# A bucketed attention with two feed-forward layers: the first head pair scores into borrowed banks, under a new order of the work

## The chip, the cores and the metric

The kernel runs on one core of one Trainium2 chip. A core has five engines that work side by side: TensorE (PE) multiplies matrices, VectorE (DVE) and ScalarE (ACT) work element by element and read its results from the PSUM banks, GpSimd (POOL) works element by element in SBUF alone in this kernel, and SyncE (SP) issues the transfers. The metric is the device time of one launch in microseconds (us), lower is better.

## The reference, cut to what matters

```python
# q, k, v: (2, 8, 768, 64); proj: (64, 6)
q_bits = (np.einsum('bhsd,dk->bhsk', q, proj) > 0)      # k_bits alike
q_bucket = np.sum(q_bits * 2 ** np.arange(6), axis=-1)  # k_bucket alike
mask = q_bucket[:, :, :, None] == k_bucket[:, :, None, :]
scores = np.where(mask, (1 / np.sqrt(64)) * q @ k.T, -1e9)
attn = np.exp(scores - scores.max(-1, keepdims=True))
attn = attn / (attn.sum(-1, keepdims=True) + 1e-09)
x = (attn @ v)                       # heads side by side: (1536, 512)
h = x @ w_in                         # first layer, d_ff 2048
x = (h * (1 / (1 + np.exp(-h)))) @ w_out
out = ((x @ w1) * (x @ w2)) @ w3 @ w_out2    # second layer, d_ff 1024
```

## The kernel before, in words

**Attention.** The 16 heads are taken as 8 pairs. For each head there are NQ = 6 groups of 128 queries against 768 keys. A group has four steps. TensorE scores it into a score tile of two PSUM banks (`scores`, L772, and `scores_lone`, L782, for the first pair, where `lone` is true and where one call scores the same group of both heads). VectorE takes the negated maximum (`peak`, L792), ScalarE exponentiates into `P` and sums the rows into a column of `sums` (`exp`, L797), and VectorE transposes `P` in blocks of 32 (`swap`, L817). When all twelve groups of a pair are transposed, TensorE weights V with them in six steps (`weigh`, L830) that take all four single banks, two called W and two called R, and the result is moved out (`move`, L849). The row sums go over TensorE (`flip`, L865), ScalarE (`unload`, L868) and VectorE (`invert`, L872) to DRAM and back as a row for every partition, and `norm` (L892) multiplies by it.

**Banks.** There are eight PSUM banks. Two score tiles of two banks each are the pool S (L381 and L382). The two tiles `turn` are the pool R (L380 and L383): the sign projections, the flips and half of the weighting use them. The two tiles `acc` are the pool W (L384): the products of the combined weights, the early steps of the first layer, half of the weighting, and 24 fillers (`warm`, L583) of three transpositions each, which compute nothing and only keep TensorE at work. After the last pair `hand_over` (L970) closes the attention's pools and gives six more banks to W.

**Weights.** Each weight comes as 64-bit words in loads of 512 KB and is made into a pair of rounded value and rest by `low`, `high`, `join`, `hi` and `lo` (`piece`, L416). During the attention w3 and the last output matrix are multiplied into one (`product`, L914): eight matrices in eight steps each, of three matmuls each.

**Layers.** `rise` and `fall` are the steps of the two layers, three matmuls each; 24 rising and 8 falling steps of the first layer are done during the attention, all others after it.

**The order.** Nothing is issued as the code is written. Each `op` call records an operation with its engines, its dependencies, the buffers it takes and gives back, and a number of the list PLACE: the first call takes the first number and so on (L254). `Plan.run` (L263) then plays the operations through with assumed durations and issues, on each engine, the one that can start first; among several of these the one with the smallest number. Buffers of S are given out in the order of the numbers, those of W and R to whoever comes (`FREE_FOR_ALL`, L241).

Of the kernel before, what the change touches and what calls it, by code (L numbers as in the profile page):

```python
# [37 lines left out]
WINDOWS = ((0, 1), (1, 1), (2, 2), (3, 2), (4, 2))  # L38
WARM, WARM_GAP = 24, 1.6
# [3 lines left out]
    220, 21, 22, 23, 19, 24, 28, 29, 90, 101, 53, 93, 91, 248, 325, 328, 326, 46, 48, 50, 43, 124, 128, 210, 199, 223,  # L43
    224, 221, 225, 17, 49, 11, 31, 18, 4, 8, 240, 13, 171, 191, 275, 348, 68, 14, 2, 232, 243, 242, 0, 6, 1, 57, 5, 132,
    9, 552, 7, 186, 45, 97, 163, 263, 121, 394, 164, 293, 125, 200, 168, 302, 129, 304, 54, 3, 241, 185, 38, 519, 245,
    116, 95, 270, 122, 689, 271, 123, 295, 318, 153, 333, 267, 170, 264, 190, 300, 197, 280, 201, 189, 208, 188, 211,
    137, 133, 203, 265, 829, 460, 234, 247, 148, 294, 515, 244, 246, 235, 60, 126, 127, 400, 414, 207, 425, 438, 173,
    175, 26, 27, 317, 327, 103, 104, 99, 96, 15, 71, 179, 182, 288, 277, 365, 363, 368, 369, 135, 174, 331, 154, 339,
    209, 337, 161, 298, 268, 334, 213, 251, 284, 338, 214, 413, 283, 379, 229, 407, 336, 381, 238, 352, 146, 344, 383,
    236, 372, 347, 384, 256, 395, 350, 393, 359, 392, 354, 399, 360, 450, 358, 420, 373, 434, 361, 426, 375, 447, 405,  # L50
    355, 464, 343, 310, 512, 1122, 586, 1129, 592, 1034, 607, 158, 144, 377, 314, 977, 290, 518, 534, 228, 155, 205,
    349, 353, 215, 206, 1077, 70, 452, 257, 269, 330, 291, 176, 222, 282, 279, 409, 401, 237, 233, 230, 231, 181, 262,
    487, 485, 415, 402, 634, 638, 631, 629, 459, 378, 429, 382, 443, 380, 430, 387, 457, 386, 445, 397, 568, 404, 453,
    412, 391, 406, 463, 417, 533, 418, 478, 441, 547, 106, 437, 483, 461, 467, 431, 496, 455, 1069, 440, 498, 465, 320,
    475, 504, 462, 1217, 486, 505, 466, 664, 491, 508, 477, 690, 490, 633, 489, 650, 591, 659, 590, 670, 570, 680, 628,
    691, 411, 469, 422, 494, 538, 863, 819, 830, 312, 82, 621, 872, 877, 136, 342, 1266, 134, 507, 296, 219, 289, 509,
    306, 305, 520, 517, 666, 661, 319, 376, 322, 316, 484, 456, 555, 482, 763, 751, 1085, 1088, 1100, 1098, 332, 497,
    530, 479, 597, 492, 554, 480, 617, 502, 559, 511, 470, 510, 569, 563, 651, 500, 574, 564, 444, 579, 587, 565, 436,
    56, 571, 580, 585, 667, 581, 602, 624, 656, 605, 606, 644, 558, 609, 674, 647, 543, 654, 688, 648, 693, 665, 706,
    702, 695, 432, 39, 802, 37, 780, 40, 812, 52, 811, 55, 1474, 59, 476, 748, 261, 677, 982, 149, 915, 934, 20, 1807,  # L60
    167, 1064, 1066, 195, 458, 1056, 341, 733, 421, 10, 906, 1052, 506, 499, 626, 622, 166, 774, 216, 192, 165, 193,
    632, 794, 699, 701, 752, 845, 852, 850, 870, 873, 44, 681, 719, 703, 760, 678, 708, 716, 791, 683, 734, 723, 827,
    726, 747, 861, 825, 729, 754, 867, 856, 728, 766, 880, 841, 107, 757, 782, 893, 789, 758, 798, 919, 732, 736, 785,
    898, 657, 761, 801, 972, 370, 779, 807, 974, 542, 772, 817, 1047, 710, 876, 945, 875, 949, 838, 965, 1619, 984,
    1638, 999, 1846, 1013, 1111, 1126, 797, 687, 892, 76, 1472, 1482, 759, 1120, 1238, 1495, 1497, 366, 523, 778, 2124,
    1394, 1193, 809, 1726, 1755, 764, 859, 718, 712, 1157, 1148, 427, 424, 416, 423, 1102, 1001, 810, 744, 1276, 1382,
    671, 673, 639, 669, 813, 796, 818, 1048, 840, 828, 885, 1357, 1167, 832, 901, 1440, 777, 831, 890, 1446, 755, 835,
    904, 1459, 1026, 866, 921, 1513, 1042, 16, 902, 960, 1514, 851, 905, 967, 1526, 1171, 912, 990, 1547, 998, 918, 993,
    1542, 324, 938, 996, 1549, 1242, 929, 1023, 1621, 1227, 1007, 1859, 1073, 1967, 1067, 1979, 1092, 1991, 1090, 2009,
    1005, 2000, 1220, 1831, 981, 844, 1104, 1632, 1453, 1470, 1620, 983, 1589, 2021, 2017, 620, 776, 578, 1006, 1596,  # L70
    1605, 2102, 1624, 1174, 1492, 1247, 846, 843, 1499, 1488, 942, 944, 927, 936, 1527, 1391, 1270, 1264, 2263, 1984,
    1375, 1367, 1124, 1125, 1780, 953, 1025, 1622, 971, 957, 1061, 1704, 1168, 966, 1070, 1715, 911, 973, 1065, 1705,
    903, 989, 1071, 1769, 1286, 1003, 1083, 1752, 1260, 1703, 1008, 1093, 1796, 1194, 1011, 1105, 1799, 1268, 1017,
    1399, 1827, 1246, 1015, 1429, 1813, 1080, 1033, 1431, 1828, 446, 1021, 1441, 1868, 641, 969, 1366, 1019, 1401, 2294,
    1400, 2242, 1411, 2233, 1427, 1068, 1438, 1853, 1854, 73, 963, 1086, 398, 1805, 1818, 1215, 922, 1493, 2527, 2590,
# [1280 lines left out]
```

## Time and profile before

| | |
|---|---|
| median of 3 runs | 714.15 us (712.88 to 716.6) |
| the profiled execution's own time | 713.73 us |
| its span, first to last instruction | 711.9 us |
| TensorE busy | 679.1 us, 95% |
| VectorE busy | 531.2 us, 75% |
| ScalarE busy | 375.4 us, 53% |
| mean granted clock of TensorE | 0.969 |

The times of the parts below are those of the profiled execution. A busy share says how much of a stretch an engine had an instruction running; matmuls overlap, so a busy TensorE need not be at its peak. The granted clock is the share of TensorE's 2.4 GHz that it was given; 0.50 is 1.2 GHz. In rows of the trace PE is TensorE's matmuls and PEld its weight loads, a bracket gives the idle time of the engine before the first instruction of the row and what ended it.

### The profile page before, as it was taken

How to read it: one execution, taken by the hardware profiler on the slowest of the kernel's cores; microseconds unless marked ns; L12 is line 12 of the kernel's file. 1: busy time of each engine (PE TensorE's matmuls, PEld its weight loads, DVE VectorE, ACT ScalarE, POOL GpSimd, SP SyncE). 2: the span in 40 equal slices, each digit the busy share in tenths (PEclk: the TensorE clock that was granted, in tenths of full speed). 3: DMA queues.
4: the chain of work that ended last, by engine and by line, in shares of the span. 5: the costliest groups of instructions: out<-in, count | busy, mean ns of one | idle time of the engine just before them, and what ended most of it. 6: DMA issues, size and time to landing. Idle time of an engine off the chain costs nothing.

```text
span 711.9 us, 14222 instructions
## 1 busy us (share of the span) xinstructions
PE 679.1 (95%) x5792; PEld 551.2 (77%) x5792; DVE 531.2 (75%) x744; ACT 375.4 (53%) x694; POOL 249.5 (35%) x243
## 2 busy tenths in 40 slices
PE   8699797999999999899999999999999999999997
PEld 5477586777887887678888888888888888878886
DVE  7887988888796996797876788687877446483555
ACT  5664866565675785465753545444735465231220
POOL 3735776586754631347020040005321043020000
PEclk9869699999999999999999999999999999999999
DMA  8444766475563563200340231102200041100004
GB/s 261 135 158 141 193 175 168 128 182 164 165 171 97 140 190 115 89 1 1 102 133 2 90 117 58 33 31 89 60 29 1 1 147 46 44 1 1 0 16 162
DMA packets 22881, 68.33 MB, mean 96 GB/s; under 512 B 3872, under 2 KB 4640, under 8 KB 22304
## 3 DMA queue, kind: packets, MB, share of 16 engines
q1 hardware_dynamic: 22816, 67.43, 31.7%
q8 instruction: 45, 0.74, 0.4%
q14 instruction: 20, 0.16, 0.1%
HBM read 55.58 MB, written 5.29 MB: 86 GB/s over the span
## 4 chain that ended last, share of the span: by engine, by line
PE 54%; DVE 4%; ACT 1%; issue 0%
PE more L1245 21%; PE more L1081 13%; PE more L1201 7%; PE acc L1081 6%; PE acc L1245 4%; PE acc L1201 3%; DVE y L407 1%; DVE gl L407 1%; DVE X L1264 1%; DVE X L1020 0%; ACT y L400 0%; DVE sg L1147 0%; ACT gh L400 0%; ACT xm L442 0%; DVE more L1098 0%
## 5 line engine op out<-in xcount | busy, mean ns | idle before, releaser
L1081 PE MATMUL more<-y,piece 128*128 128x512 f32 x432 | 110.0, 389 | 0.0
L799 ACT ACTIVATE P<-score,st 128x768 f32<-128x768 f32 x96 | 85.7, 896 | 45.1 <-DVE st L793 42.7
L793 DVE TENSOR_REDUCE st<-score 128x1 f32<-128x770 f32 x96 | 88.0, 946 | 24.2 <-PE score L777 20.6
L1245 PE MATMUL more<-gh,piece 128*128 128x512 f32 x312 | 105.3, 389 | 0.1
L1264 DVE SCALAR_TENSOR_TENSOR X<-more,X 128x512 f32<-128x512 f32 x101 | 68.2, 687 | 39.3 <-PE more L1245 38.7
L818 DVE STREAM_TRANSPOSE pt<-P 128x768 f32<-128x768 f32 x96 | 90.0, 964 | 9.0 <-ACT P L799 8.6
L1081 PEld LDWEIGHTS more<-y,piece 128*128 128x128 f32 x432 | 81.1, 188 | 16.9
L836 PE MATMUL turn<-pt,V 32*64 32x193 f32 x1536 | 74.9, 334 | 5.1 <-issue 5.1
L836 PE MATMUL acc<-pt,V 32*64 32x193 f32 x1536 | 75.9, 334 | 2.8 <-issue 2.6
L836 PEld LDWEIGHTS acc<-pt,V 32*64 32x64 f32 x1536 | 59.3, 134 | 11.9 <-issue 9.5
L1245 PEld LDWEIGHTS more<-gh,piece 128*128 128x128 f32 x312 | 58.6, 188 | 12.6 <-DVE X L1264 0.5
L836 PEld LDWEIGHTS turn<-pt,V 32*64 32x64 f32 x1536 | 56.7, 134 | 7.7 <-issue 7.1
L457 DVE SCALAR_TENSOR_TENSOR x<-x,x 128x512 uint32<-128x512 uint32 x60 | 48.4, 810 | 17.2 <-ACT x L442 16.6
L1245 PE MATMUL more<-gl,piece 128*128 128x512 f32 x156 | 60.8, 390 | 0.4 <-DVE gl L407 0.4
L777 PE MATMUL score<-ka,qa 128*128 128x384 f32 x168 | 51.4, 389 | 8.6 <-ACT P L799 7.6
L1201 PE MATMUL more<-x,piece 128*128 128x512 f32 x216 | 55.0, 389 | 0.0
L1081 PE MATMUL acc<-y,piece 128*128 128x512 f32 x198 | 52.8, 391 | 0.1
L447 ACT ACTIVATE x<-raw 128x512 uint32<-128x512 uint32 x43 | 28.9, 673 | 38.8 <-DVE piece L407 16.4
L918 PE MATMUL acc<-piece,piece 128*128 128x512 f32 x192 | 48.9, 397 | 0.4 <-ACT X L855 0.4
L777 PEld LDWEIGHTS score<-ka,qa 128*128 128x128 f32 x168 | 30.1, 204 | 23.6 <-ACT P L799 14.3
L1245 PE MATMUL more<-piece,gh 128*128 128x512 f32 x152 | 47.1, 391 | 0.4 <-DVE sg L1098 0.2
L1201 PEld LDWEIGHTS more<-x,piece 128*128 128x128 f32 x216 | 40.5, 188 | 8.4
(191 smaller groups left out, 1338.6 us busy)
## 6 DMA issues: line engine op xcount, KB each, us to landing
raw<-in_w SPq DMA_DIRECT2D x25, 512.0 KB
raw<-in_wo SPq DMA_DIRECT2D x22, 512.0 KB
raw<-in_win SPq DMA_DIRECT2D x15, 512.0 KB
V<-in_v SPq DMA_DIRECT2D x16, 384.0 KB
rawm<-in_w SPq DMA_DIRECT2D x7, 512.0 KB
kraw<-in_kT SPq DMA_DIRECT2D x8, 384.0 KB
qraw<-in_qT SPq DMA_DIRECT2D x8, 384.0 KB
invb<-inverse SPq DMA_DIRECT2D x16, 192.0 KB
```

The lines of the kernel that those rows point to most:

```text
L447: nc.scalar.activation(out=u32(t), in_=pair(raw)[:, :, 0], func=AF.Copy, scale=0.875 * 2.0 ** -29, bias=0.49)
L457: engine[e].scalar_tensor_tensor(out=u32(x), in0=u32(x), scalar=3, in1=u32(t), op0=ALU.logical_shift_left, op1=ALU.bitwise_or)
L777: nc.tensor.matmul(out=sc[:, g, :HF], lhsT=lhs[:k, qs], rhs=rhs[:k, g * HF:g * HF + HF], start=(k == 128), stop=(k != 128),)
L793: nc.vector.tensor_reduce(out=plan[uk("st")][:, 0:1], in_=plan[uk("S")][:, :, :HF + 1], op=ALU.max, axis=AX.XY, negate=True)
L799: nc.scalar.activation(out=plan[uk("P")], in_=plan[uk("S")][:, :, :HF], func=AF.Exp, bias=s[:, 0:1], accum_out=plan[key("sums")][:, par * ...
L818: nc.vector.transpose(plan[mine][:, :, 32 * i:32 * i + 32], plan[uk("P")].rearrange("p g (b i) -> p (g b) i", i=32))
L836: nc.tensor.matmul(out=to[a][64 * side:64 * side + 64, :GW + 1], lhsT=V[rows_, c, side], rhs=plan[key(f"pt{side}")][rows_, c, :GW + 1], st ...
L918: nc.tensor.matmul(out=plan[key + ("ps",)], lhsT=w[:, a, k], rhs=r[:, c], start=(k == 0 and n == 0), stop=(k == 7 and n == 2),)
L1081: nc.tensor.matmul(out=plan[bk[b]], lhsT=w[:, a], rhs=y, start=(opens and j == 0 and m == 0), stop=(j == 1 and m == 2), skip_group_check=True)
L1201: nc.tensor.matmul(out=plan[key], lhsT=w[:, a], rhs=x, start=(k == 0 and n == 0), stop=(k == 3 and n == 2))
L1245: nc.tensor.matmul(out=plan[key], lhsT=a, rhs=x, start=(f == 0 and n == 0), stop=(f == 1 and n == 2))
L1264: nc.vector.scalar_tensor_tensor(out=dst, in0=plan[key], scalar=by, in1=dst, op0=ALU.mult, op1=ALU.add)
```

## The change: four borrowed banks, the inverse in columns, another list

The first pair's groups 1 and 3 (of 0 to 5) no longer take a score tile. `turn` and `acc` are allocated as two tiles of two banks each; their halves serve as R and W, and for these two groups the first head's scores take both halves of `turn`, the second head's both halves of `acc`. After the exponentials of both groups an operation without an instruction, `set_apart`, closes the two tiles and opens four tiles of one bank in their place. Column 384 of each half of the new areas is set to a large negative number at the start, as in the score tiles, since `peak` reads 385 columns.

The row sums are inverted before they are transposed, as 128 x 12 instead of 12 x 128, with the small constant added on VectorE instead of by ScalarE's bias. `invert` is declared with 260 ns instead of 850.

PLACE has one number more and is new from the first to the last. Some of its numbers, in the order of the first pair's calls: setup 220 before and 0 after; the fillers 21 to 328 before and 17 to 235 after; the six `scores_lone` 0, 5, 7, 163, 164, 168 before and 28, 33, 48, 86, 93, 123 after; the first head's `swap` 57, 552, 97, 394, 200, 304 before and 51, 56, 84, 113, 124, 143 after; `weigh` 267, 264, 300, 280, 189, 188 before and 158, 167, 171, 185, 191, 205 after; `invert` 829 before and 169 after; `hand_over` 12 before and 1257 after.

```diff
+BESIDE = (1, 3)
...
 PLACE = [
-    220, 21, 22, 23, 19, 24, 28, 29, 90, 101, 53, 93, 91, 248, 325, 328, 326, 46, 48, 50, 43, 124, 128, 210, 199, 223,
...
-    2220, 2260,
+    0, 17, 24, 67, 74, 76, 70, 64, 80, 79, 83, 109, 111, 112, 115, 120, 131, 127, 139, 148, 155, 220, 228, 235, 233, 2, 3,
...
+    2889, 2896, 2949, 2890, 2897,
 ]
...
-    wps, ps = pool("wps", PSUM), pool("ps", PSUM, st)
+    lent_banks = ctx.enter_context(ExitStack())
+    acc_pool, ps = pool("accs", PSUM, lent_banks, "right"), pool("ps", PSUM, st)
+    turn_pool = pool("turns", PSUM, lent_banks)
...
-    turns = tiles(ps, "turn", [128, 512], F32, 2)
+    acc = acc_pool.tile([128, 2, 512], F32, name="acc2")
+    turn = turn_pool.tile([128, 2, 512], F32, name="turn2")
     score_tiles = tiles(ps, "score", [128, 2, 512], F32, 2)
     plan.buffers("S", score_tiles)
-    plan.buffers("R", turns)
-    plan.buffers("W", tiles(wps, "acc", [128, 512], F32, 2))
+    plan.buffers("R", [turn[:, i] for i in range(2)])
+    plan.buffers("W", [acc[:, i] for i in range(2)])
...
-        for s in score_tiles:
+        for s in (*score_tiles, turn, acc):
             nc.vector.memset(s[:, :, HF:HF + 1], -BIG / 2)
...
+                lent_out = lone and i in BESIDE
+                space = [("RW"[par], uk(("S", x))) for x in range(2)] if lent_out else [("S", uk("S"))]
+
+                def area(u=u):
+                    return plan["S", "u", u] if ("S", "u", u) in plan.held else (turn, acc)[u // NQ]
...
-                                      [("S", (x, "u", v)) for x in ("S",) for v in ((u, u + NQ) if lone else (u,))])
+                                      [(p, (x, "u", v)) for v, q in (((u, "R"), (u + NQ, "W")) if lone else ((u, "S"),))
+                                       for p, x in ([(q, ("S", y)) for y in range(2)] if lent_out else [("S", "S")])])
...
+                beside += [ex] if lent_out else []
...
+            if lone and par == 1:
+
+                def set_apart(e, key=key):
+                    lent_banks.close()
+                    banks = {"W": tiles(pool("wps", PSUM, side="right"), "acc", [128, 512], F32, 2), "R": tiles(pool("tps", PSUM, st), "turn", [128, 512], F32, 2)}
+                    for p in "WR":
+                        for i in range(2):
+                            plan.held[key(f"old{p}{i}")] = p, banks[p][i]
+
+                olds = [(p, key(f"old{p}{i}")) for p in "WR" for i in range(2)]
+                op({"": 0}, set_apart, beside, tu + 1, olds, [x for _, x in olds])
...
+                def invert(e, key=key):
+                    x = plan[key("sums")]
+                    nc.vector.tensor_scalar(out=x, in0=x, scalar1=(S + 1e-9) * FLOOR, scalar2=1.0, op0=ALU.add, op1=ALU.mult)
+                    nc.vector.reciprocal(out=x, in_=x)
...
                 def unload(e, key=key):
-                    nc.scalar.activation(out=plan[key("invt")][:2 * NQ, :128], in_=plan[key("it")][:2 * NQ, :128], func=AF.Copy,
-                                         bias=(S + 1e-9) * FLOOR)
-
-                def invert(e, key=key):
-                    x = plan[key("invt")][:2 * NQ, :128]
-                    nc.vector.reciprocal(out=x, in_=x)
-
-                fl = op({"PE": 110}, flip, pair_exps, te + 3, [("R", key("it"))], [key("sums")])
-                un = op({"ACT": act(128)}, unload, [fl], te + 3.5, [("wsb", key("invt"))], [key("it")])
-                iv = op({"DVE": 850}, invert, [un], te + 4)
+                    scaled(e, plan[key("invt")][:2 * NQ, :128], plan[key("it")][:2 * NQ, :128])
+
+                iv = op({"DVE": 260}, invert, pair_exps, te + 3)
+                fl = op({"PE": 110}, flip, [iv], te + 3.5, [("R", key("it"))], [key("sums")])
+                un = op({"ACT": act(128)}, unload, [fl], te + 4, [("wsb", key("invt"))], [key("it")])
...
-                        [iv], te + 8, give=[key("invt")], size=6144, kind="send")
+                        [un], te + 8, give=[key("invt")], size=6144, kind="send")
```

## Rows read from the trace of the kernel before

**Rows 1.** The page's busy us, share of the span and instructions of each engine.

```profile
PE 679.1 (95%) x5792; PEld 551.2 (77%) x5792; DVE 531.2 (75%) x744; ACT 375.4 (53%) x694; POOL 249.5 (35%) x243
```

**Rows 2.** Windows of the whole core: stretch, then the columns named in the first line.

```profile
core 0: us, PE busy (x) PEld busy (x) DVE busy (x) ACT busy (x) POOL busy (x), PEclk, DMA share, GB/s
10.00:45.00 35.00, 27.00 (x158) 19.12 (x160) 30.64 (x36) 22.68 (x42) 21.87 (x18) 0.78 0.59 183
45.00:50.00 5.00, 5.00 (x23) 3.58 (x15) 3.72 (x5) 2.96 (x7) 0.58 (x1) 0.53 0.05 9
50.00:88.00 38.00, 31.64 (x465) 25.24 (x465) 31.09 (x38) 24.83 (x47) 25.88 (x24) 0.81 0.62 176
88.00:152.00 64.00, 59.09 (x959) 46.53 (x958) 53.41 (x66) 40.95 (x79) 44.39 (x38) 0.95 0.57 153
152.00:288.00 136.00, 129.30 (x2312) 106.37 (x2312) 111.97 (x138) 89.22 (x177) 66.95 (x59) 1.00 0.55 155
290.00:708.00 418.00, 417.06 (x1828) 342.84 (x1827) 292.63 (x446) 188.82 (x334) 88.91 (x96) 1.00 0.15 51
```

**Rows 3.** Timeline of VectorE, first pair: start us, us, operation, count, idle before.

```profile
10.12 1.83 DVE L793 TENSOR_REDUCE st<-score 128x1 f32<-128x770 f32 x2
19.99 1.83 DVE L793 TENSOR_REDUCE st<-score 128x1 f32<-128x770 f32 x2 [0.75 <-PE score L789]
34.76 1.83 DVE L793 TENSOR_REDUCE st<-score 128x1 f32<-128x770 f32 x2 [1.47 <-PE score L789]
41.00 1.83 DVE L793 TENSOR_REDUCE st<-score 128x1 f32<-128x770 f32 x2 [1.19 <-PE score L789]
43.08 1.86 DVE L818 STREAM_TRANSPOSE pt<-P 128x768 f32<-128x768 f32 x2 [0.25 <-ACT P L799]
```

**Rows 4.** Waits of VectorE from 10 to 45 us: us in total, times, longest.

```profile
DVE st L793 <- PE score L789: 3.4, 3, 1.5
DVE pt L818 <- ACT P L799: 0.8, 3, 0.3
```

**Rows 5.** Timeline of TensorE around 30 us.

```profile
30.62 0.69 PE L789 MATMUL score<-x 64*128 64x384 f32 x1 [4.33 <-ACT P L799]
```

**Rows 6.** Windows of 10 us of the whole core, columns as in rows 2.

```profile
20.00:30.00 10.00, 5.17 (x40) 3.94 (x40) 9.75 (x10) 5.60 (x9) 8.49 (x5) 0.96 0.51 150
30.00:40.00 10.00, 8.96 (x39) 6.44 (x39) 7.92 (x10) 6.96 (x15) 4.57 (x5) 0.50 0.55 189
80.00:90.00 10.00, 7.89 (x57) 5.84 (x65) 9.06 (x12) 7.84 (x13) 6.40 (x7) 0.50 0.75 221
```

**Rows 7.** Windows of the fillers (L585): matmuls, weight loads, clock, DMA.

```profile
10.00:45.00 35.00, 10.04 (x60) 8.06 (x60) 0.78 0.59 183
```

**Rows 8.** Groups by line: busy us, mean ns of one; then VectorE's timeline at 65 us.

```profile
L874 DVE RECIPROCAL wsb<-wsb 12x128 f32<-12x128 f32 x8 | 7.4, 930 | 3.3 <-ACT wsb L869 3.3
L857 DVE TENSOR_SCALAR X<-acc,fv 128x192 f32<-128x192 f32 x6 | 2.2, 413 | 0.1
...
65.32 0.16 DVE L402 COPY fv<-acc 128x1 f32<-128x1 f32 x1 [0.51 <-PE turn L836]
```

**Rows 9.** Timeline of VectorE: first and last rows of six joins after 10.12 us.

```profile
11.87 0.68 DVE L457 SCALAR_TENSOR_TENSOR x<-x,x 128x512 uint32<-128x512 uint32 x1
...
38.88 0.94 DVE L457 SCALAR_TENSOR_TENSOR x<-x,x 128x512 uint32<-128x512 uint32 x1
```

**Rows 10.** Timeline of TensorE at 50 us.

```profile
50.07 0.39 PE L836 MATMUL acc<-pt,V 32*64 32x193 f32 x4
```

**Rows 11.** Windows of the products (L918): matmuls, weight loads, clock, DMA.

```profile
45.00:88.00 43.00, 6.03 (x24) 4.40 (x24) 0.78 0.55 157
```

**Rows 12.** Timeline of VectorE at 60 us.

```profile
59.85 1.83 DVE L793 TENSOR_REDUCE st<-score 128x1 f32<-128x770 f32 x2 [3.97 <-PE score L777]
```

**Rows 13.** Timeline of TensorE at 151 us.

```profile
151.29 1.07 PE L836 MATMUL acc<-pt,V 32*64 32x193 f32 x6
```

More of the change, by code (lines that the diff above doesn't have):

```diff
@@ L360, in lsh_attention_moe_kernel, with pool @@
     op = plan.op
-    def pool(name, space=None, stack=ctx):
+    def pool(name, space=None, stack=ctx, side=None):
         kw = {} if space is None else {"space": space}
+        kw |= {"side": side} if side else {}
         return stack.enter_context(tc.tile_pool(name=name, bufs=1, **kw))
@@ L566, in setup @@
             nc.gpsimd.memset(x[:, :, GW:], FLOOR)
-        warm = turns[0]
         for _ in range(18):
-            nc.tensor.transpose(warm[:, :128], ident, ident)
+            nc.tensor.transpose(turn[:, 0, :128], ident, ident)
     def place_tiled(e):
@@ L757, in lsh_attention_moe_kernel @@
                  give=[] if lone else [key("qraw"), key("kraw"), key("bits")])
-        both, evicted, moves, spreads, pair_exps = {}, {}, [], [], []
+        both, evicted, moves, spreads, pair_exps, beside = {}, {}, [], [], [], []
         for par in range(2):
@@ L767, in lsh_attention_moe_kernel, with scores @@
                 uk = lambda x, u=u: (x, "u", u)
+                lent_out = lone and i in BESIDE
+                space = [("RW"[par], uk(("S", x))) for x in range(2)] if lent_out else [("S", uk("S"))]
+                def area(u=u):
+                    return plan["S", "u", u] if ("S", "u", u) in plan.held else (turn, acc)[u // NQ]
                 mine = key(f"pt{par}")
                 qs = slice(i * 128, i * 128 + 128)
-                def scores(e, hk=hk, uk=uk, qs=qs):
-                    sc = plan[uk("S")]
+                def scores(e, hk=hk, qs=qs, area=area):
+                    sc = area()
                     for lhs, rhs, k in (("qa", "ka", 128), ("qb", "kb", 64 + 2 * NB)):
@@ L788, in scores_lone, with peak, exp @@
                                 k = slice(64 * side, 64 * side + 64) if p < 3 else slice(32 * side, 32 * side + 2 * NB)
-                                nc.tensor.matmul(out=plan["S", "u", side * NQ + i][:, g, :HF], lhsT=lhs[k, qs],
+                                nc.tensor.matmul(out=area(side * NQ + i)[:, g, :HF], lhsT=lhs[k, qs],
                                                  rhs=rhs[k, g * HF:g * HF + HF], start=(p == 0), stop=(p == 3))
-                def peak(e, uk=uk):
+                def peak(e, uk=uk, area=area):
                     nc.vector.tensor_reduce(
-                        out=plan[uk("st")][:, 0:1], in_=plan[uk("S")][:, :, :HF + 1], op=ALU.max, axis=AX.XY, negate=True
+                        out=plan[uk("st")][:, 0:1], in_=area()[:, :, :HF + 1], op=ALU.max, axis=AX.XY, negate=True
                     )
-                def exp(e, uk=uk, key=key, i=i, par=par):
+                def exp(e, uk=uk, key=key, i=i, par=par, area=area):
                     s = plan[uk("st")]
                     nc.scalar.activation(
-                        out=plan[uk("P")], in_=plan[uk("S")][:, :, :HF], func=AF.Exp, bias=s[:, 0:1],
+                        out=plan[uk("P")], in_=area()[:, :, :HF], func=AF.Exp, bias=s[:, 0:1],
                         accum_out=plan[key("sums")][:, par * NQ + i:par * NQ + i + 1],
@@ L813, in lsh_attention_moe_kernel @@
                 ex = op({"ACT": 890}, exp, [pk, *pair_exps[:1]], tu - 2.7,
-                        [("P", uk("P"))] + ([("sums", key("sums"))] if i == 0 and par == 0 else []), [uk("S"), uk("st")])
+                        [("P", uk("P"))] + ([("sums", key("sums"))] if i == 0 and par == 0 else []), [*(x for _, x in space), uk("st")])
                 pair_exps.append(ex)
+                beside += [ex] if lent_out else []
                 def swap(e, uk=uk, mine=mine, i=i):
```

2 lines of the change are left out of this document (1 added, 1 removed), and 289 rows, old and new, of the table PLACE.

## The prediction

> **What bounds the kernel now.** I read the page's busy shares first. TensorE is busy for 95% of the span, VectorE for 75%, ScalarE for 53% [rows 1]. A share over the whole span mixes stages, so the next view is the span in stretches, cut where the work changes [rows 2]. From 290 to 708 us TensorE is busy 417.06 of 418 us at a granted clock of 1.00: that part is TensorE's own work, 0.94 us of it idle, and no order can shorten it much. From 152 to 288 us it is the same but for 6.7 us idle. Up to 152 us it is different: of the four stretches between 10 and 152 us TensorE is idle in 8.0, 0, 6.4 and 4.9 us, together 19.3 us, and its clock is 0.78, 0.53, 0.81 and 0.95. A granted clock of 0.50 is the lower of its two levels, 1.2 against 2.4 GHz, so a mean of 0.78 over 35 us means some 15 us at the low level; over the four stretches it comes to 15.4 + 4.7 + 14.4 + 6.4 = 41 us. VectorE is idle there in 4.4, 1.3, 6.9 and 10.6 us, 23.1 us in all. So what can be won lies before 152 us, and after that TensorE hands any gain or loss through to the end nearly whole.
>
> Why the opening is slow is seen on VectorE. Its path through the first pair runs from the first maximum at 10.12 us to the end of the last transposition at 43.08 + 1.86 = 44.94 us. On it the maxima at 19.99, 34.76 and 41.00 us wait 0.75, 1.47 and 1.19 us for scores [rows 3], 3.4 us in all, and three transpositions 0.8 us for exponentials [rows 4]. The scores wait in turn for the exponentials to leave the two score tiles: TensorE stands for 4.33 us before the group at 30.62 us [rows 5]. That pause and the stretch around it, 5.17 of 10 us busy, are followed by a clock of 0.50 from 30 to 40 us [rows 6].
>
> **The change part by part.** *Two more score areas.* Groups two and four of the first pair (the loop's 1 and 3) no longer wait for the exponentials of the group before, since they have their own four banks. What that can give is bounded by VectorE: of its path only the 3.4 us are waits for scores. I take them whole, because a group's matmuls can now run while VectorE works on the group before; the bounds are 0 (the waits come back) and the 4.2 us of both kinds of wait.
>
> *Their price.* While these two groups hold the R and W banks, the filler transpositions, which need W, cannot run: 60 of the 72 lie in this stretch, 10.04 us of TensorE time [rows 7]. They compute nothing, so losing cover costs only through the clock; that is the third rival below. The two memsets added to the setup lie beside the identity's making and cost nothing; if that cover were gone it would be a VectorE copy of one column each, 0.16 us [rows 8]. The second pair's sign projection needs an R bank. The list puts it between the second and the fourth group, so it is not behind both. The taking apart issues no instruction; it asks that exponentials of both groups be done before the banks are used singly, which delays nothing that the list puts before it.
>
> *The order.* The number list is new throughout, and it can be read. Pairing each number with its operation, in the old list 4,235 of 10,309 dependencies run against the numbers, in the new one 9. So the new list stands nearly in order of time. From it: ahead of the last transposition of the first pair stand three joins of split weights beside one put before the first maximum, where the trace has six after it [rows 9]. Those three joins come later, so they shorten this path by 3 x 0.68 = 2.0 us but are owed back at once in the second pair's stretch: I count nothing. Then, in the trace the first weighting starts at 50.07 us [rows 10], 5.1 us after its last input was there. TensorE is busy for all of 45 to 50 us, at 0.53 [rows 2], with the second pair's scores, two transposed products and fillers. In the new list the weighting comes straight after the last transposition with two score groups of the second pair ahead instead of three, and the projection and the sums' transposition behind it. That work is only moved, but if it runs later at the full clock it takes 5.0 x 0.53 = 2.65 us instead of 5.0 us. I take the difference, 2.35 us, between 0 (the clock stays low) and 5.0 us (hidden wholly).
>
> The old order puts the first product of the combined weights into the second pair's stretch: 24 matmuls, 6.03 us between 45 and 88 us [rows 11]. The new one puts it behind the second pair's weighting, and up to the fourth pair's both orders have the same 32 product steps, and 146 VectorE steps on either list. It is moved, not saved. At full clock it is at most 6.03 us of the 6.4 us that TensorE idles from 50 to 88 us anyway, and the next stretch has 4.9 us idle to take it in: I count nothing, and price it in the second rival.
>
> *The inverse in columns.* Before, the sums are transposed, evacuated and inverted as 12 x 128, 0.93 us on VectorE for each of eight pairs [rows 8]. After, an add and an inversion work on 128 x 12 and the transposition follows. The trace has no 12-column operation on VectorE. It is between the copy of one column (0.16 us) and the 192-column add (0.413 us) for the add, and between 0.16 and 0.93 us for the inversion. Being much nearer to one column I take 0.17 + 0.38 = 0.55 us, a saving of 0.38 us a pair, bounds -0.41 and +0.61. TensorE's transposition and ScalarE's evacuation stay one each. Only the three pairs up to 152 us count: 1.1 us (-1.2 to 1.8); later VectorE is not the bound [rows 2].
>
> *After 152 us* the new list has the same counts ahead of each weighting as the old (231 VectorE steps ahead of the seventh, 274 ahead of the eighth, 24 rising and 8 falling steps of the first layer), and seven falling steps instead of six between the last weighting and the first step that needs the banks handed over. I count 0, with a loss of a few microseconds as bound, since 0.94 us idle leaves nothing to win.
>
> **Sum.** 3.4 + 2.35 + 1.1 = 6.9 us. The profiled execution took 713.73 us (span 711.9 and 1.8 around it), so 706.8; it lies 0.4 us under the runs' median of 714.15, which makes 707.2. I say 707.0. All upper bounds, 4.2 + 5.0 + 1.8 us, give 703; if the new order also fills half of the 6.9 us that VectorE idles from 50 to 88 us, for instance the 3.97 us before the maxima at 59.85 us that stand behind the weighting's burst [rows 12], it is 699.5. The lower bounds, 0 + 0 - 1.2, give 715.4.
>
> The Trainium skill, page "TensorE: Matmul & The Clock Gate", Part 1, says that the low clock is the default and that only activity lifts it. The trace agrees, 0.50 after the pause above. By that rule the change speaks against itself, since it takes fillers and a product out of the opening, and its result is the third rival's 719 instead of 707.
>
> **The rivals.** *Given back.* The first pair ends earlier, but TensorE has no product to fill the second pair's stretch and the 6.03 us are missing later, where 4.9 us are idle at most. If 5.3 us of them (6.03 at a part-low clock) fall on TensorE's path, 1.6 us remain: 712.5. For it: from 88 us on TensorE is busy 59.09 of 64 us. Against it: the second pair's stretch should be shorter by what is moved out.
>
> *The change does not do what it says.* The wide tiles are also written by fillers and the projection; if the extra groups wait for these, or VectorE's order has no maximum ready, the 3.4 us stay. Then 2.35 + 1.1 us remain at best, 710.7, or 1.1 alone, 713.
>
> *Slower: the clock.* Fillers blocked by held banks and no product in the second pair's stretch leave TensorE idle there, and the clock goes low for longer. Low time costs half its length wherever TensorE is the bound, as it is from 88 us on (6.4 us low now). If 24 us of low clock more fall on such work, the cost is 12 us, and with the 6.9 us gained the time is 719. It decides from 14 us on, where gain and cost are even. For it: two drops at 30 and 80 us already [rows 6]. Against it: the dense weighting comes right after the first pair, and a low clock that lies in VectorE's stretch is hidden.
>
> *The long rest in a new order.* 417.06 of 418 us busy can only get worse. If some twenty inputs each came 0.3 us late, 6 us would go: 713.
>
> **How the numbers follow.** Measured differences under 0.5%, 3.6 us, cannot be told from none here, as the three runs span 3.7 us. So faster ends at 710.6 and slower begins at 717.7. The forecast's case with its higher gains has 0.60. Given back, not done, or eaten by the long rest: 0.26, of which 0.03 still falls under 710.6. The clock: 0.14, with 0.13 above 717.7 and the rest below. That makes faster 0.63, same 0.24, slower 0.13. The range runs from the case with all gains, 699.5, up to 717, where the second and fourth rivals and their lower bounds are inside and most of the clock's is left out. The likeliest case alone runs from 699.5 to 711.
>
> **What would show it.** Right: no maximum of the first pair waits for scores; its last transposition ends near 40 us, the first weighting starts near 42; the fourth pair's weighting, at 151.29 us now [rows 13], starts near 145; TensorE stays as dense as before from there on; the inversion on VectorE takes a third to a half of its time. Wrong: waits for scores in the first pair as long as now, a clock low for much of 45 to 100 us, new idle time on TensorE after 152 us, or a weighting of the fourth pair no earlier than now.

## The result: slower by 0.5%

The changed kernel takes 720.58 us in the median of 20 runs against 716.39 us before, ratio 1.0053 [1.0028, 1.0078]. The forecast was 707.0 us, in a range from 699.5 to 717.0. The profiled execution that came with the result ran at a clock of 0.742 over 845.9 us and says nothing of the change, so the profile after is that of a second run of the changed kernel (median 717.88 us, ratio 1.0051 [1.0023, 1.008]; the profiled execution took 719.78 us, span 718.0 us, clock 0.969).

Windows of the changed kernel, which answer to [rows 2], with the rest cut finer:

```profile
core 0: us, PE busy (x) PEld busy (x) DVE busy (x) ACT busy (x) POOL busy (x), PEclk, DMA share, GB/s
10.00:45.00 35.00, 27.99 (x339) 21.49 (x341) 30.18 (x38) 24.61 (x46) 22.53 (x21) 0.85 0.55 174
45.00:50.00 5.00, 5.00 (x156) 4.24 (x138) 3.30 (x5) 3.10 (x8) 3.15 (x3) 1.00 0.18 66
50.00:88.00 38.00, 33.17 (x553) 24.87 (x545) 33.43 (x44) 26.50 (x54) 27.57 (x24) 0.82 0.63 182
88.00:152.00 64.00, 56.16 (x796) 45.30 (x795) 54.84 (x66) 43.46 (x84) 43.92 (x40) 1.00 0.61 180
205.00:245.00 40.00, 34.77 (x673) 28.17 (x672) 34.09 (x43) 23.94 (x46) 19.04 (x15) 0.91 0.42 115
290.00:340.00 50.00, 45.11 (x183) 35.66 (x182) 37.80 (x49) 21.91 (x41) 23.68 (x23) 0.93 0.06 23
```

The same windows of the kernel before, where they were not among [rows 2]:

```profile
205.00:245.00 40.00, 38.63 (x639) 31.29 (x638) 32.89 (x39) 26.29 (x52) 25.17 (x20) 1.00 0.46 124
290.00:340.00 50.00, 49.54 (x212) 40.06 (x212) 43.11 (x59) 29.38 (x54) 29.14 (x26) 0.98 0.06 22
```

Up to 152 us the clock is higher or equal everywhere: that of 45 to 50 us is 1.00 instead of 0.53, that of 88 to 152 us 1.00 instead of 0.95, though other profiles of the same list have 0.95 to 1.00 there. The losses stand in two places that the forecast had put down as settled. From 205 to 245 us TensorE is busy 3.9 us less, at 0.91 instead of 1.00, and from 290 to 340 us 4.4 us less, at 0.93 instead of 0.98. Both come again in later profiles of the same order: 33.9 and 35.2 us busy in the first stretch (the evacuation moved, and the cut behind the eighth pair, below), 44.9 to 45.4 us in the second (old list then new, the norm moved, the evacuation moved). From 340 to 700 us the two kernels are within 0.8 us, 358.74 and 359.52 us busy.

The starts of the weightings say when the time is won and lost. These are rows of TensorE's timeline in the changed kernel, the first, fourth, sixth, seventh and eighth pair's first weighting, and the last row of the eighth's:

```profile
39.86 0.39 PE L859 MATMUL acc<-pt,V 32*64 32x193 f32 x4
143.93 0.39 PE L859 MATMUL acc<-pt,V 32*64 32x193 f32 x4
208.92 0.88 PE L859 MATMUL acc<-pt,V 32*64 32x193 f32 x6
238.44 0.60 PE L859 MATMUL acc<-pt,V 32*64 32x193 f32 x4
273.89 0.72 PE L859 MATMUL acc<-pt,V 32*64 32x193 f32 x6 [0.24 <-DVE kraw L1170]
284.54 0.61 PE L859 MATMUL turn<-pt,V 32*64 32x193 f32 x6
```

The same for the sixth to the eighth pair before:

```profile
217.96 0.39 PE L836 MATMUL acc<-pt,V 32*64 32x193 f32 x4
240.26 0.96 PE L836 MATMUL acc<-pt,V 32*64 32x193 f32 x6
275.35 1.02 PE L836 MATMUL acc<-pt,V 32*64 32x193 f32 x5
287.67 0.56 PE L836 MATMUL turn<-pt,V 32*64 32x193 f32 x5
```

With [rows 10, 13] the lead of the changed kernel is 10.2 us at the first pair, 7.4 at the fourth and 9.0 at the sixth. One pair later it is 1.8 us, and at the last row of the last weighting 3.1 us. Part of the 9.0 us is only a shift: ahead of the sixth weighting stand 77 maxima before and 74 in the changed kernel, while it is 51 in both ahead of the fourth and 84 and 85 ahead of the seventh. Compared like with like, the lead falls from 7.4 to 1.8 us between the fourth pair and the seventh. Behind that last row, the changed kernel takes 718.0 - 284.5 = 433.5 us to the end and the kernel before 711.9 - 287.7 = 424.2: a lead of 3.1 becomes an arrears of 6.1 us, which is the difference of the two spans. These are single executions; by the ratio of many the loss is 0.5%, 3.7 us.

**The first place, 228 to 240 us.** VectorE's timeline in the changed kernel:

```profile
232.34 2.52 DVE L917 TENSOR_TENSOR X<-X,invb 128x768 f32<-128x768 f32 x1 [1.32 <-DMA invb<-inverse]
234.78 0.94 DVE L803 TENSOR_REDUCE st<-score 128x1 f32<-128x770 f32 x1
```

TensorE's, at the same time, then a row of ScalarE's:

```profile
233.26 0.59 PE L787 MATMUL score<-ka,qa 128*128 128x384 f32 x2 [2.06 <-issue]
...
236.86 1.01 PE L787 MATMUL score<-ka,qa 128*128 128x384 f32 x2 [2.65 <-ACT P L809]
```

```profile
232.17 0.90 ACT L809 ACTIVATE P<-score,st 128x768 f32<-128x768 f32 x1
```

A norm (L917, the product with the spread inverse sums) stands on VectorE between two maxima. In the list it is the fifth pair's, issued behind the sixth's; the expectations below call it the sixth's. It waits 1.32 us for the copy of the inverse sums and then runs for 2.52 us, so the next maximum starts at 234.78 us with its scores already there. TensorE waits 2.65 us for the exponential behind that maximum. The 2.06 us ahead of it are not the norm's: those scores start at 233.26 us, when the exponential of 232.17 us and the reading of its sum are over at 233.16 us, and ScalarE had come to it late, after three other steps from 229.18 us on. This wait stands in the same place when the norm is gone from there (below).

**The second place, the hand-over of the banks.** TensorE's waits from 290 to 440 us in the changed kernel, then VectorE's timeline ahead of the longest:

```profile
PE more L1268 <- DVE X L1287: 5.7, 3, 4.5
```

```profile
308.25 1.79 DVE L412 TENSOR_TENSOR y<-X,y 128x512 fp32r<-128x512 f32 x1
309.96 1.77 DVE L412 TENSOR_TENSOR gl<-kraw,gh 128x512 fp32r<-128x512 f32 x1
...
313.94 3.50 DVE L1043 TENSOR_TENSOR X<-X 128x512 f32<-128x512 f32 x3
317.37 1.21 DVE L412 TENSOR_TENSOR y<-X,y 128x512 fp32r<-128x512 f32 x1
...
319.70 0.68 DVE L1287 SCALAR_TENSOR_TENSOR X<-more,X 128x512 f32<-128x512 f32 x1
```

The evacuation that frees a bank for the falling product (L1287) comes at 319.70 us, and from 306 us up to it VectorE is never idle. Its steps of 128x512 with both inputs in SBUF take 0.68 us alone, as at 318.50 us, and 1.2 to 1.8 us here. Beside them stand GpSimd's sums (L503, and L513 up to 318.0 us):

```profile
307.73 3.46 POOL L503 TENSOR_TENSOR sum<-piece 128x512 f32<-128x512 f32 x2
```

Before, TensorE has one wait from 290 to 440 us, of 0.4 us. The slowed steps alone are not the difference: the kernel before has two of 1.78 and 1.77 us at 307 and 309 us, beside GpSimd's differences.

### The profile page after: what moved, and what is told of

Same layout as the page of the kernel before. It is cut to its first block, busy times and chain, and to the rows that moved or that the text cites. A ratio compares the mean times of both kernels' runs of the same rounds, so it can differ in the third digit from the quotient of the medians.

```text
span 845.9 us, 14204 instructions
## 1 busy us (share of the span) xinstructions
PE 821.5 (97%) x5792; PEld 590.5 (70%) x5792; DVE 537.0 (63%) x759; ACT 372.4 (44%) x682; POOL 251.4 (30%) x250
## 4 chain that ended last, share of the span: by engine, by line
PE 91%; DVE 4%; ACT 2%; issue 2%; DMA 1%; POOL 0%; ACTq 0%; DVEq 0%; POOLq 0%
PE more L1268 20%; PE more L1104 13%; PE more L1224 10%; PE score L787 9%; PE acc L1268 8%; PE acc L859 8%; PE acc L1104 7%; PE acc L941 6%; PE acc L1224 4%; PE turn L859 2%; ACT P L809 1%; DVE st L803 1%; PE score L799 1%; PE acc L589 1%; PE turn L647 1%
## 5 line engine op out<-in xcount | busy, mean ns | idle before, releaser
L1104 PE MATMUL more<-y,piece 128*128 128x512 f32 x408 | 127.0, 456 | 0.0
L1287 DVE SCALAR_TENSOR_TENSOR X<-more,X 128x512 f32<-128x512 f32 x91 | 62.3, 689 | 78.3 <-PE more L1268 78.2
L859 PE MATMUL turn<-pt,V 32*64 32x193 f32 x1536 | 93.2, 403 | 4.8 <-issue 4.8
L859 PE MATMUL acc<-pt,V 32*64 32x193 f32 x1536 | 93.1, 400 | 0.8 <-issue 0.7
L1224 PE MATMUL more<-x,piece 128*128 128x512 f32 x252 | 78.1, 455 | 0.0
L859 PEld LDWEIGHTS turn<-pt,V 32*64 32x64 f32 x1536 | 68.0, 150 | 7.9 <-issue 7.7
L1104 PE MATMUL acc<-y,piece 128*128 128x512 f32 x222 | 72.0, 456 | 0.0
L409 POOL TENSOR_SCALAR piece<-x 128x512 fp32r<-128x512 f32 x35 | 23.3, 668 | 141.0 <-DVE x L462 58.7
L941 PE MATMUL acc<-piece,piece 128*128 128x512 f32 x192 | 58.6, 457 | 0.0
L1104 PEld LDWEIGHTS acc<-y,piece 128*128 128x128 f32 x222 | 44.1, 199 | 18.9
L787 PE MATMUL score<-kb,qb 76*128 76x384 f32 x168 | 52.4, 401 | 0.0
```

The source lines that it names most:

```text
L409: engine[e].tensor_scalar(out=dst, in0=src, scalar1=by, scalar2=1.0, op0=ALU.mult, op1=ALU.mult)
L787: nc.tensor.matmul(out=sc[:, g, :HF], lhsT=lhs[:k, qs], rhs=rhs[:k, g * HF:g * HF + HF], start=(k == 128), stop=(k != 128),)
L859: nc.tensor.matmul(out=to[a][64 * side:64 * side + 64, :GW + 1], lhsT=V[rows_, c, side], rhs=plan[key(f"pt{side}")][rows_, c, :GW + 1], st ...
L941: nc.tensor.matmul(out=plan[key + ("ps",)], lhsT=w[:, a, k], rhs=r[:, c], start=(k == 0 and n == 0), stop=(k == 7 and n == 2),)
L1104: nc.tensor.matmul(out=plan[bk[b]], lhsT=w[:, a], rhs=y, start=(opens and j == 0 and m == 0), stop=(j == 1 and m == 2), skip_group_check=True)
L1224: nc.tensor.matmul(out=plan[key], lhsT=w[:, a], rhs=x, start=(k == 0 and n == 0), stop=(k == 3 and n == 2))
```

## The experiments

From the second experiment on, the planner's due times (PLACE) are replaced by a fixed list of operations with their engines, in order of issue, so that a list of one kernel can be joined to the banks or the inverse of the other. In the diffs such a list is written in names. It holds the planner's own order on every engine, so that a kernel differs from its model by the edit named, and at most by the place of one TensorE step in the first pair besides. Every ratio is against the kernel before, timed beside it on the same chip.

**The changed kernel again.** No edit.

> The changed kernel once more, for a trace at the full clock and a ratio on the chip of the next three. All theories: 0.3 to 0.8% slower than before. The order theory (the new list loses what the banks win): no wait for scores in the first pair, its last transposition before 42 us, but new idle or low-clock time of TensorE of 8 us or more, before 290 us. The clock theory (held banks keep the fillers out): the granted clock from 10 to 88 us lower than 0.78, 0.53, 0.81 by enough to cost 8 us. The long-rest theory: 5 us or more of idle time on TensorE after 290 us.

717.88 us, 1.0051 [1.0023, 1.008]: the loss is there again, and this is the profile shown above.

**One part at a time.** The changed kernel's list with the old banks and the inverse in rows:

```diff
-BESIDE = (1, 3)
-invert on sums [128 x 12], then flip, unload
+flip, unload, then invert on [12 x 128]
 order: the changed kernel's
```

> The order of issue of the changed kernel, with the banks and the inverse of the kernel before; groups two and four of the first pair are scored as soon as a score tile is free. Order theory: 1.0 to 2% slower than before, since it keeps the loss and lacks the 3.4 us. Clock theory: within 0.5% of before, since no bank is held. Long-rest theory: 0.7 to 1.3% slower, with the idle time after 290 us as in the changed kernel.

738.8 us, 1.0356 [1.031, 1.0402]. VectorE's waits from 10 to 53 us:

```profile
DVE st L784 <- PE score L780: 15.5, 6, 5.3
```

This is more than any theory had. Without the borrowed banks the maxima of the new list wait 15.5 us for scores instead of 3.4 [rows 4]; the last transposition of the first pair ends at 52.87 us. The rows cost this list as well, as the last experiments show.

The old list with the borrowed banks, groups two and four issued right behind the group ahead:

```diff
+BESIDE = (1, 3)
 order: the kernel's before, but
+scores_lone 0, scores_lone 1, ... scores_lone 2, scores_lone 3
```

> The order of issue of the kernel before, with the four borrowed banks: groups two and four of the first pair are scored right behind the group ahead, fillers and projections where their bank is free. Order theory: the waits for scores go, 0.2 to 0.6% faster than before. Clock theory: 0.5% or more slower, with a lower clock before 88 us. Long-rest theory: 0 to 0.5% faster.

722.19 us, 1.0116 [1.007, 1.0161]. TensorE's waits from 10 to 56 us, then VectorE's:

```profile
PE acc L580 <- ACT P L800: 8.8, 1, 8.8
PE turn L638 <- ACT P L800: 5.5, 1, 5.5
```

```profile
DVE st L794 <- PE score L790: 8.2, 3, 5.1
```

The held banks stop TensorE at a filler (L580) for 8.8 us and at the second pair's sign projection (L638) for 5.5 us, and the scores queued behind these come later than without the banks: 8.2 us of waits instead of 3.4. The clock theory had the sign right and not the reason: the clock up to 88 us is 0.76, 0.57 and 0.86 here, against 0.78, 0.53 and 0.81.

The old list with the inverse in columns, at the place where the transposition of the sums stood:

```diff
-flip, unload, invert [12 x 128]
+invert [128 x 12], flip, unload
```

> The order of issue of the kernel before, with the sums inverted in columns ahead of their transposition, at the transposition's old place. All theories: within 0.3% of before. VectorE's part 0.4 to 0.6 us a pair in place of 0.93 us; each inversion may hold VectorE up for a few tenths of a microsecond until the last exponential.

724.48 us, 1.0126 [1.0077, 1.0174]. TensorE's waits from 10 to 290 us hold a line that the kernel before does not have:

```profile
PE turn L862 <- DVE sums L859: 8.0, 6, 2.5
```

The transposition of the sums now needs VectorE's inverse. In a list that was made for the other way round, TensorE stands there for 8.0 us, in six waits. No theory had that.

So each part alone, at the one place tried for it, is slower by 1.2 to 3.6%, and the three together by 0.5%.

**Where the loss lies.** The changed kernel's list to the last weighting of the sixth pair, then what is left in the old order, and the reverse:

```diff
 order: the changed kernel's to the sixth pair's last weighting
-order: the changed kernel's from there
+order: the kernel's before from there
```

> The changed kernel up to the last weighting of the sixth pair, and from there the remaining operations in the order of the kernel before. Theory of two places (the opening's gain is real and two stalls of the new order after 205 us eat it): the sixth pair's weighting starts near 209 us as in the changed kernel, the 4.5 us wait at the hand-over goes, and the time is 0.8 to 1.4% under before. Rival (the time is bound by how soon the weights arrive, and an earlier head only waits later): within 0.4% of before, with new idle time on TensorE after 220 us.

> The kernel before up to the last weighting of the sixth pair, and from there the remaining operations in the order of the changed kernel, with the banks and the inverse of before. Theory of two places: the stalls come without the gain, 1.2 to 2.4% slower than before. Rival: within 0.5% of before.

New then old: 713.75 us, 0.9961 [0.9933, 0.9988]. Old then new: 727.45 us, 1.0177 [1.014, 1.0214]. The new list wins in the first six pairs and loses in the rest, whatever stands ahead of it. The gain is smaller than the theory's 0.8 to 1.4% and no larger than its rival allowed; the last of the cuts below decides between them. In the reverse the same wait returns (TensorE from 205 to 440 us):

```profile
PE more L1236 <- DVE X L1255: 5.7, 3, 4.5
```

The cut at the sixth pair is no clean one: the first of the two kernels stands 4.1 us at the eighth pair's weighting, where the kernel before stands 3.0 and the changed kernel 1.9 us, and another 2.7 us in the seventh pair's.

**The norm moved.** The norm of 232 us goes from VectorE to GpSimd, nothing else:

```diff
-norm (pair 5) on DVE
+norm (pair 5) on POOL, behind the second difference that follows
```

> The changed kernel with one operation moved: the sixth pair's normalisation, which stands on VectorE at 232 us for 1.3 us waiting and 2.5 us running ahead of a maximum, goes to GpSimd behind the last pair's rests. Theory of two places: TensorE's idle 4.7 us from 230 to 240 us shrinks to under 2.5 us, the time falls by 2 to 5 us against the changed kernel, to between 0.3% faster and 0.3% slower than before. Rival (the pause there is made by the scores' operands): TensorE still idle 4 us or more, 0.4 to 0.8% slower than before.

715.26 us, 0.999 [0.9963, 1.0016], 0.6% below the changed kernel. TensorE's waits from 205 to 245 us:

```profile
PE score L778 <- issue: 2.0, 1, 2.0
```

The wait of 2.65 us for the exponential is gone, and the one ahead of it, behind ScalarE's steps, stays. The wait of 4.5 us at the hand-over is still there.

**The evacuation moved.** The evacuation that TensorE waits for at 320 us is issued four steps earlier in VectorE's order, ahead of the last differences:

```diff
+evacuation (L1287), right behind its product
 differences, folds
-evacuation (L1287)
```

> The changed kernel with one operation moved: on VectorE, the evacuation for which TensorE waits 4.5 us at 320 us goes ahead of the differences that stand before it. Theory of two places: that wait falls under 1.5 us, and with it the low clock after it; 3 to 7 us less than the changed kernel, between 0.5% faster and 0.1% slower than before. Rival (VectorE's backlog only moves on): another wait of 3 us or more shortly after, time as the changed kernel.

717.91 us, 1.0041 [1.0014, 1.0068]. TensorE's waits from 290 to 440 us:

```profile
PE acc L1259 <- ACT X L396: 3.0, 1, 3.0
PE more L1259 <- DVE X L1278: 2.3, 3, 1.0
```

The wait of 4.5 us falls to 1.0, and one of 3.0 us for ScalarE takes its place. So this one step, moved alone, wins nothing that the ratio shows; which of the steps around it cost the time was not tried one by one.

**The cut behind the eighth pair.** The old order takes over only after the last weighting; then the same with the norm moved as well:

```diff
 order: the changed kernel's to the eighth pair's last weighting
+norm (pair 5) on POOL            (second kernel alone)
-order: the changed kernel's from there
+order: the kernel's before from there
```

> The changed kernel's list of issue up to the last weighting of the eighth pair, then what is left in the order of before. Theory (the new order loses in two separate places, some 7 us between the sixth and the seventh pair and some 9 us after the last weighting, and the second is an order of VectorE's steps at the hand-over): the last weighting ends at 284 to 286 us as in the changed kernel, the wait of 4.50 us at the hand-over goes, TensorE is busy for 49 of the 50 us from 290 to 340 us, and what follows the last weighting takes 424 to 428 us as before: span 709 to 713, ratio 0.991 to 0.997. Rival (a cut anywhere costs: steps that one list had put back and the other had not yet done pile up behind it, as at the eighth pair of the earlier cut): new idle time of 4 us or more within 30 us of the cut, span 714 or more, ratio 0.998 or above.

> The same as the kernel cut at the eighth pair, with the sixth pair's norm issued on GpSimd in place of VectorE. Theory (VectorE's norm holds up the maxima between 228 and 240 us): the seventh pair's first weighting starts 2 to 3 us earlier than with the cut alone, at 235 to 236 us, TensorE's stretch of low clock from 230 to 240 us goes, and the time is 2 to 4 us below the cut alone: span 706 to 710, ratio 0.987 to 0.993. Rival (GpSimd is late as well, and what waits for the norm only moves): within 1.5 us of the cut alone, seventh weighting at 238 us or later, ratio within 0.002 of it.

713.43 us, 0.9967 [0.9934, 1.0], and with the norm moved 709.36 us, 0.9916 [0.988, 0.9952]: the second is faster than both kernels. Its windows:

```profile
205.00:245.00 40.00, 37.55 (x855) 31.13 (x854) 34.87 (x48) 25.84 (x50) 17.73 (x14) 0.96 0.41 118
290.00:340.00 50.00, 49.58 (x217) 40.14 (x216) 42.51 (x60) 28.43 (x53) 26.62 (x26) 1.00 0.04 16
```

From 290 to 340 us TensorE is busy 49.58 us again. GpSimd's sums of the pieces, and the evacuations ahead of them on VectorE, in this kernel:

```profile
312.55 3.50 POOL L494 TENSOR_TENSOR sum<-piece 128x512 f32<-128x512 f32 x2
```

```profile
309.87 1.27 DVE L1278 SCALAR_TENSOR_TENSOR X<-more,X 128x512 f32<-128x512 f32 x2
...
311.90 0.68 DVE L1278 SCALAR_TENSOR_TENSOR X<-more,X 128x512 f32<-128x512 f32 x1
```

In the old order three evacuations stand ahead of those sums, from 309.87 us on, at about 0.65 us each; in the new one the sums start at 307.73 us and the evacuation comes 12 us after. That this is what costs the time is not shown, since no run moves the sums alone. The seventh pair's weighting now follows the sixth's after 26.4 us (204.85 and 231.27 us), with the cut alone after 29.9 us (208.74 and 238.60 us). So the order of what follows the last weighting is worth 1.0051 - 0.9967 = 0.84%, 6.0 us, and the norm 0.51%, 3.7 us, each to within some 3 us by the intervals. Of the 6.0 us, 4.5 show in TensorE's busy time from 290 to 340 us. The last row of the last weighting starts at 278.18 us, and 426.9 us follow it, against 424.2 us before: 2.7 us more, for which no run gives the cause.

**The rows back.** The changed kernel's banks and list with the inverse in rows, first right behind the evacuation of the sums, then three VectorE steps later:

```diff
-invert [128 x 12], flip, unload
+flip, unload, invert [12 x 128]                   (first)
+flip, unload, three VectorE steps, invert [12 x 128]   (second)
```

> The changed kernel with its banks and its order, and the sums inverted in rows again, on VectorE behind the evacuation. Theory (the columns are worth what they take off VectorE up to the fourth pair, three times 0.58 us, and nothing later): 1 to 2.5 us slower than the changed kernel, ratio 1.007 to 1.009. Rival (the columns' price is TensorE, which stands at the transposition of the sums until VectorE has inverted them, 8.0 us in six waits when the columns stood in the order of before, 1.6 us in two in the changed kernel): with rows no wait of the transposition for VectorE, the eighth pair's weighting 1 to 2 us earlier, and 1 to 2 us faster than the changed kernel, ratio 1.002 to 1.004.

> The kernel with rows back, with each of the eight inversions three VectorE steps later than right behind ScalarE's evacuation of the sums, all else as in that kernel. Theory (the rows cost because VectorE stands in its order for the evacuation, 4.1 us in five waits after 50 us, and not because the operation itself is longer): these waits fall under 1 us in all and most of the loss goes: ratio 1.004 to 1.012, near the changed kernel's 1.005. Rival (the place is not it: the inverse's copies through memory are late for the norms, or TensorE's transposition and the evacuation of the sums fall at bad places in an order made without them): the waits go and the ratio stays at 1.018 or above.

732.56 us, 1.0229 [1.0176, 1.0283], and 735.64 us, 1.0307 [1.0264, 1.0349]. Neither theory of the first had it so dear, and that of the second fell. The first differs from the order alone (1.0356) only by the banks and the place of one score step. So to this list the banks are worth 1.0356 - 1.0229 = 1.3%, 9 us, and the columns 1.0229 - 1.0051 = 1.8%, 13 us, each to within some 5 us by the intervals. VectorE's waits from 50 to 290 us in the first hold this line:

```profile
DVE wsb L888 <- ACT wsb L883: 4.1, 5, 1.7
```

In the second it is gone, and TensorE and ScalarE wait instead (same stretch, to 300 us for TensorE):

```profile
PE acc L850 <- ACT wsb L396: 6.9, 4, 4.3
```

```profile
ACT wsb L396 <- DMA inverse<-wsb: 6.5, 3, 2.2
```

In rows the evacuated sums lie in a wsb buffer until they are inverted and sent away. Inverted at once, VectorE waits for the evacuation; inverted later, ScalarE waits for the buffer and TensorE for ScalarE. In columns the inverse is done before the buffer is taken. These waits are shown; that they make up the whole 13 us between the first kernel and the changed one is not, since TensorE's waits for exponentials grew as well, from 3.9 to 5.4 us between 88 and 152 us.

## Why the prediction was wrong

**The failed step is "After 152 us the new list has the same counts ahead of each weighting as the old ... I count 0".** In order of issue the counts are the same but for one VectorE step (231 and 232 ahead of the seventh weighting, 274 and 275 ahead of the eighth), and they were the wrong measure. What changed is which engine a step is on and what stands next to it. The norm on VectorE cost 3.7 us (the norm moved behind the cut; 0.6% when it alone was moved), the order behind the last weighting 6.0 us (the cut behind the eighth pair). Both places were in the forecast as a bound of "a few microseconds"; together they are 9.7 us. Without them the kernel is 6.0 us faster than before, with them 3.7 us slower. Which steps at the hand-over cost the 6.0 us stays open. The sentence "0.94 us idle leaves nothing to win" was right, and is just why it should have weighed more: a stretch that dense can only lose. The forecast's own sign of being wrong, "new idle time on TensorE after 152 us", is what the windows show.

**The opening was right in its result.** The first weighting was forecast near 42 us and stands at 39.86; the fourth pair's near 145 us and stands at 143.93. The time that the sum gives, 6.9 us less than before, is near what the cut with the norm moved shows, in which the two later places are mended: 0.84%, 6.0 us [3.4, 8.6]. That agreement is partly luck, since its terms were off. The lead of 10.2 us at the first weighting is 5.7 us of VectorE's path and 4.7 us of the gap behind it, less 0.2 us of a later start:

- *Score waits, 3.4 us taken whole.* They fall less. VectorE's timeline of the changed kernel, which answers to [rows 3], then a row of TensorE's:

```profile
12.66 0.95 DVE L803 TENSOR_REDUCE st<-acc 128x1 f32<-128x770 f32 x1
...
25.18 0.96 DVE L803 TENSOR_REDUCE st<-turn 128x1 f32<-128x770 f32 x1 [2.09 <-PE acc L799]
...
32.61 1.25 DVE L462 SCALAR_TENSOR_TENSOR x<-x,x 128x512 uint32<-128x512 uint32 x2
...
37.62 0.96 DVE L803 TENSOR_REDUCE st<-score 128x1 f32<-128x770 f32 x1 [0.64 <-PE score L787]
38.49 0.97 DVE L830 STREAM_TRANSPOSE pt<-P 128x768 f32<-128x768 f32 x1
```

```profile
18.66 4.70 PE L589 MATMUL acc<-ident 128*128 128x128 f32 x24
```

The second group's maxima (in acc and turn) wait for nothing. The fourth group's wait 2.09 us, because TensorE runs a burst of fillers, 4.70 us from 18.66 us on, in one of their own banks and ahead of those scores. So 3.4 becomes 2.1 us, a gain of 1.3.
- *The joins, "2.0 us ... owed back at once ... I count nothing".* They carry most of the gain. From the first maximum to the last transposition VectorE's path is 34.8 us before and 38.49 + 0.97 - 10.32 = 29.1 us now, 5.7 less. Six joins and three splits, 6.5 + 2.2 us, became three joins of 1.9 us, and one maximum of the second pair moved in, 0.96 us behind a wait of 0.64 us. They are owed back, but not at once: of the 10.2 us at the first weighting 7.4 are left at the fourth; that the joins are what is paid there is not shown.
- *The gap ahead of the weighting, 2.35 us.* Too small: from the last transposition to the first weighting it is 5.1 us before and 39.86 - 39.46 = 0.4 us now, 4.7 us less, near the bound of 5.0 us for work that is hidden wholly. The clock of 45 to 50 us is 1.00, but with the weighting in that stretch it says nothing of this term.
- *Columns, 0.55 us a pair.* Wrong, though the wait that they remove was not in the sum either. The eight additions and inversions of the changed kernel, with the least, the median and the longest duration in ns:

```profile
L890 DVE TENSOR_SCALAR sums<-sums x8: 122/604/1564, 41.7 to 272.0; 128x12 f32<-128x12 f32 x8
L891 DVE RECIPROCAL sums<-sums x8: 227/228/230, 42.1 to 272.2; 128x12 f32<-128x12 f32 x8
```

The inversion is below its forecast of 0.38 us. The addition takes 0.12 us free and up to 1.56 us, in the mean 0.73 (5.9 us in eight), so that both together take 0.96 us, as long as the row form's 0.93 [rows 8]. So what the columns are worth to this list, 13 us, is not their running time; the waits that came with the rows are a part of it.

**The rivals.** *The clock* fell: in all profiles of the changed list with its banks and columns the clock up to 152 us is higher than before or equal. The fillers in the opening are 54 instead of 60, not few. *Given back* fell in the main: the first pair's product moved on to 87.46 us, and 7.4 us of lead stand at the fourth pair. *Does not do what it says* came half true: 2.1 of the 3.4 us stay, behind fillers, as it said; the path is shorter all the same. *The long rest in a new order* was the right one, with its place too vague and its price of 6 us too low: the order behind the last weighting alone cost 6.0 us, the norm 3.7 more, and in a few long waits (4.5 and 2.65 us) instead of twenty of 0.3 us. It stood at 713 us, on the side of no change, though its own mechanism had no ceiling there. The slower side should have been this rival.

A count in the working is off, and nothing hangs on it: of the new list's 10,313 dependencies one runs against the numbers, not nine.

## What to carry to other kernels

A list of issue that is new throughout is not a change of the opening, whatever it is for: compare the new place of each engine's steps against the old wherever the bounding engine has no idle time left, above all which steps move to another engine and which two engines' steps come side by side. A step's count before a milestone says nothing of that. Where one stretch gains and another loses, join the lists at a place with no half-done work and take the better half of each: here the join gave a ratio of 0.9967, and with one norm moved 0.9916, from a list at 1.0053.

## What was not expected of the hardware

VectorE and GpSimd hold each other up. At the hand-over VectorE's 128x512 differences take 1.79 and 1.77 us beside two GpSimd sums of together 3.46 us, and 0.68 us alone; GpSimd's 128x256 sums take 1.19 us there, and 0.74 us at 316.12 us in the cut kernel. The norm on VectorE takes 2.52 us while GpSimd runs its differences, and 0.96 us in the kernel before. The addition on 128x12 takes 0.12 to 0.15 us when GpSimd is idle and up to 1.56 us beside it. The evacuations, which read a PSUM bank, show none of it: the two at 309.87 us in the cut kernel take 1.27 us together while GpSimd works from 310.15 to 311.44 us. Of these the smallest step suffers most in proportion, so an estimate by size alone, as for the columns, is an estimate for a free moment.

Two executions with the same list up to the fifth pair's norm differ: with the cut behind the eighth pair the last row of the fifth weighting starts at 187.8 us, with the norm moved as well at 183.9, with clocks from 88 to 152 us of 0.95 and 1.00. A difference of 4 us in one pair's place is within what two profiles of one list show, so the worth of the norm is taken from the ratios and from the distance of two weightings, not from their places.
